# Four attention layers on one core: when the side work of the full layers is queued

## The chip, the cores and the metric

The kernel runs on one core of one Trainium2 chip. The metric is the device time of one execution in microseconds (us); the kernel before was executed three times for its time and once more under the hardware profiler. The core has engines that run at the same time, each with its own instruction queue: PE (TensorE, matrix products into PSUM), ACT (ScalarE, here mostly exponentials), DVE (VectorE), POOL (GpSimd) and SP (SyncE, which issues nearly all DMAs).

## The reference

The input x is 2048 x 512 in float32. Four layers follow each other, each with layer norm, 32 heads of 16, softmax attention, an output projection and a residual sum:

```python
x = A_x
x = x + _A_ref(_layernorm(x, axis=-1), A_wqkv, A_wo)
x = x + _B_ref(_layernorm(x, axis=-1), B_wqkv, B_wo)
x = x + _A_ref(_layernorm(x, axis=-1), A_wqkv, A_wo)
x = x + _B_ref(_layernorm(x, axis=-1), B_wqkv, B_wo)
return x
```

`_A_ref` (layers 0 and 2) lets each query see the 256 keys up to itself; `_B_ref` (layers 1 and 3, the full layers) lets it see all 2048. Both compute softmax(q k / 4) v per head and multiply by their output weights.

## The kernel before

**Score pairs.** A full layer walks through chunks of 512 queries (`c`, four of them) and head groups of four heads (`qd`, eight of them). For one chunk and head group it goes through 16 tiles `j` of 128 keys. For each tile, two score products (`exps`, L663; eight matmul instructions each) fill two PSUM buffers `s`, ACT takes the exponential of each (L671, 128 x 1024), and one tile later 16 products with the values (L715) add into `acc`. So a full layer has 1024 exponentials. When a head group ends, `epilogue` (L624 on) joins, transposes and divides the sums on DVE and POOL. Layer 1 takes the chunks in turn, each with eight head groups. Layer 3 is cut into blocks `(t, c)`: quarter `t` of the heads (two head groups) and chunk `c`, `t` in the outer loop; a block has 64 exponentials. The keys and queries of a head group are read back from DRAM when it begins (`load_full`: `kt` from `kf`, `qt` from `qs`).

**Side work.** Between score pairs PE does other matmuls, which prepare what comes later: projections of keys and queries (`keys`, `queries`, through `project`: twelve side matmuls per 128 output rows), values (`values`), output projections (`wo`, and in layer 3 `wo_part`: one head quarter of one chunk, four groups of three). In a full layer all of it goes through one PSUM tile, `halves`, because the other banks hold scores and sums. A side matmul is eight instructions (L360) and counts as `MM` = 0.222 us of PE; one for half of the heads' values counts as half.

**Squares.** Softmax needs no maximum here: a bound on the scores is taken from the sums of squares of keys and of queries. After the last matmul of a projection DVE joins the two halves (L374, L375), casts (L465, L466), POOL squares (L471), and two (or eight) small matmuls with `hsum` sum the squares over each head's rows (`squares`, L490) into `halves`. DVE then makes a maximum of them for keys (`km`, L509) or a row `m` for queries (L522, L523), which a DMA writes into `qs` (L535); the `qt` load of that chunk reads it. The squares of a finished projection are not emitted at once: a function is put on the list `pend` with a due time, and `settle` emits what is on the list, all of it or only what is due. In full layers `mms` (the function that emits a group of side matmuls) settles at its start, `key_shift` settles at its start (it needs the key maxima of all four chunks and writes the shift of the keys into `kf`), and the attention loop settles at the end of every block.

**The planner.** Python code decides where side work stands in the program, with an estimated clock `clock[0]`. Each piece of side work is a `Work` with a generator, a cost, dependencies and a name; output projections of layer 3 (`O3`) and the shift of the keys (`shift3`) have no name. `Side` holds a queue of them, and always takes the first one that is ready. In a full layer `share` is called once per key tile after the first of a head group, and once more inside the second: 16 calls per head group. It adds to a budget (cost left by steps left, at least `least`, up to 0.75) and lowers `lag`, and then emits side matmuls while the budget and the lag allow it and the clock is past `PH["free"]`. `mms` sets `PH["free"]` after a group, so that DVE has time to empty `halves`. A step, one key tile, counts as at least 1.8 us. At the end of a block of layer 3, `finish` emits everything that is still in the queue, whatever the budget. The works of the next block then form a new queue, with `carried` works (until now only preparations of weights) ahead of them. The queue of a block `(t, c)` is, in order: values of the upper heads (only in chunks 2 and 3 of the first quarter and in all four of the second), queries of chunk `c+1`, keys of chunk `c` for quarter `t+1`, in the last chunk the shift of the keys and the queries of chunk 0 for quarter `t+1`, and the output projection of the chunk before.

**Checks.** `verify` (queued in layer 1 as `CW`, after the fourth head group of the first chunk) makes sure that the weights are in a range for which the arithmetic holds. For each of eight matrices it loads four pieces into one buffer `wc` (L308), and DVE reduces each (L310); the waits between are the planner's.

**What sets the order.** Only PE executes in the order of the program text:

```python
ctx.enter_context(tc.manual_schedule(engines={mybir.EngineType.PE}))
```

For DVE, ACT, POOL and SP the compiler orders the instructions itself; earlier program text gives a higher priority, and `tc.high_priority` raises it further. On the chip every queue then runs strictly in the order that came out of this.

Of the kernel before, what the change touches and what calls it, by code (L numbers as in the profile page):

```python
# [19 lines left out]
P = 128  # L20
# [168 lines left out]
def fast_path(ctx, tc, flag, a_x, a_wqkv, a_wo, b_wqkv, b_wo, out):  # L189
# [29 lines left out]
    def wait(us):  # L219

        return "wait", clock[0] + us
# [80 lines left out]
    def verify(ty, s):  # L302

        am = vp.tile([P, D], F32, name=f"wa{ty}_{s}", tag="wa", bufs=1)
        for k in range(NC):
            f = slice(k * P, (k + 1) * P)
            raw = vp.tile([P, NC, P], F32, name=f"wc{ty}_{s}_{k}", tag="wc", bufs=1)
            nc.sync.dma_start(raw, mats[ty, s][:, f].rearrange("(k p) f -> p k f", p=P))  # L308
            yield wait(6)
            nc.vector.tensor_reduce(am[:, f], raw.rearrange("p k f -> p f k"), axis=AX.X, op=ALU.max, apply_absolute_value=True)  # L310
            yield wait(3)
        at = vp.tile([P, D], F32, name=f"wt{ty}_{s}", tag="wc", bufs=1)
        nc.vector.transpose(at, am)
        mx = vp.tile([P, D // 32], F32, name=f"wx{ty}_{s}", tag="wx")
        nc.vector.tensor_reduce(mx, at.rearrange("p (b r) -> p b r", r=32), axis=AX.X, op=ALU.max)
        nc.vector.tensor_tensor(wlow, wlow, mx, ALU.min)
        nc.vector.tensor_tensor(whigh, whigh, mx, ALU.max)
        yield wait(3)
# [29 lines left out]
    def mms(ps, pairs, after=1.6, us=MM):  # L348


        if PH["full"] and pend:
            settle()
            PH["free"] = clock[0] + 1.6
            yield 0.1
        for i, (a, b) in enumerate(pairs):
            if PH["full"]:
                for g in range(0, P, 32):
                    for r in range(2):
                        k = slice(R * r, R * r + R)
                        nc.tensor.matmul(ps[g:g + 32, r], a[k, g:g + 32], b[k], start=(i == 0), stop=(i == len(pairs) - 1),  # L360
                                         skip_group_check=True)
            else:
                nc.tensor.matmul(ps, a, b, start=(i == 0), stop=(i == len(pairs) - 1))  # L363
            spent(us)
            if i < len(pairs) - 1:
                if PH["full"]:
                    yield us
            else:
                PH["free"] = clock[0] + after
    TERMS = ((0, 0), (0, 1), (1, 0))  # L370

    def join(dst, ps, scale=1 / WS):
# [61 lines left out]
    def project(l, s, c, act, ht=None):  # L434


        ty, n = l % 2, f"{l}_{s}_{c}" + ("" if ht is None else f"_h{ht}")
        w = weights(ty, s, n, *((0, D) if ht is None else (ht * P, (ht + 1) * P)))
        yield wait(8)
        xc = XC[l, c]  # L440
        if s == 0:
            dst = rows(qs[ty, c])
        elif ty == 0:
            dst = rows(kw[c])
        else:
            dst = rows(kf)[:, :, c * QC:(c + 1) * QC]
        sqs = {}
        for t in range(NHT) if ht is None else (ht,):
            ps = bank()
            w0 = t * P if ht is None else 0  # L450
            yield from mms(ps, [(w[:, k, a, w0:w0 + P], xc[:, b, k, :]) for a, b in TERMS for k in range(NC)], 2.2)
            settle(not sqs)
            sp = vp.tile([P, 2, QC], F16, name=f"sp{n}_{t}", tag="sp", bufs=3)
            with tc.high_priority(HEAD_START):
                if PH["full"]:
                    j = vp.tile([P, QC], F32, name=f"j{n}_{t}", tag="j")
                    join(j, (ps[:, 0], ps[:, 1]))
                else:
                    if act:
                        nc.scalar.activation(sp[:, 0], ps, AF.Copy, scale=1 / WS)  # L460
                    else:
                        nc.vector.tensor_scalar(sp[:, 0], ps, 1 / WS, None, op0=ALU.mult)
                    nc.vector.scalar_tensor_tensor(sp[:, 1], ps, 1 / WS, sp[:, 0], op0=ALU.mult, op1=ALU.subtract)
            if PH["full"]:
                nc.vector.tensor_copy(sp[:, 0], j)  # L465
                nc.vector.tensor_tensor(sp[:, 1], j, sp[:, 0], ALU.subtract)  # L466
            sq = vp.tile([P, QC], BF16, name=f"sq{n}_{t}", tag="sq", bufs=NHT)
            if act:
                nc.scalar.activation(sq, sp[:, 0], AF.Square)
            else:  # L470
                nc.gpsimd.tensor_tensor(sq, sp[:, 0], sp[:, 0], ALU.mult)  # L471
            sqs[t] = sq

            d = dst[8 * t:8 * t + 8].rearrange("h (d b) n -> (h d) b n", b=4)
            if s:
                nc.sync.dma_start(d[:, 0:2], sp[:, 0:1].broadcast_to([P, 2, QC]))
                nc.sync.dma_start(d[:, 2], sp[:, 1])
            else:
                nc.sync.dma_start(d[:, 0:2], sp)
                nc.sync.dma_start(d[:, 2], sp[:, 0])  # L480
            yield -MM if PH["full"] else -12 * MM
        return sqs
# [17 lines left out]
    def keys(l, c, act, ht=None):  # L500
        sqs = yield from project(l, 1, c, act, ht)

        def rest():
            ph = squares(f"k{l}_{c}_{ht}", sqs)
            if l not in KM:
                KM[l] = vp.tile([P, NQ], F32, name=f"km{l}", tag="km", bufs=2)
            r = quarters(ht)
            with tc.high_priority(HEAD_START):
                nc.vector.tensor_reduce(KM[l][r, c:c + 1], ph[r], axis=AX.XY if PH["full"] else AX.X, op=ALU.max)  # L509
        pend.append((clock[0] + 3.6, rest))  # L510

    def queries(l, c, act, ht=None):
        sqs = yield from project(l, 0, c, act, ht)

        def rest():
            ph = squares(f"q{l}_{c}_{ht}", sqs)

            m = vp.tile([P, QC], F16, name=f"m{l}_{c}_{ht}", tag="m", bufs=1)
            if l % 2:
                r = quarters(ht)  # L520
                if PH["full"]:
                    nc.vector.tensor_scalar(m[r], ph[r, 0], -0.515, None, op0=ALU.mult)  # L522
                    nc.vector.scalar_tensor_tensor(m[r], ph[r, 1], -0.515, m[r], op0=ALU.mult, op1=ALU.add)  # L523
                else:
                    nc.vector.tensor_scalar(m[r], ph[r], -0.515, None, op0=ALU.mult)
            else:
                kx = vp.tile([P, 1], F32, name=f"kx{l}_{c}", tag="kx")
                nc.vector.tensor_reduce(kx, KM[l][:, max(c - 1, 0):c + 1], axis=AX.X, op=ALU.max)
                if PH["full"]:
                    nc.vector.tensor_scalar(m, ph[:, 0], kx, -0.515, op0=ALU.add, op1=ALU.mult)  # L530
                    nc.vector.scalar_tensor_tensor(m, ph[:, 1], -0.515, m, op0=ALU.mult, op1=ALU.add)
                else:
                    nc.vector.tensor_scalar(m, ph, kx, -0.515, op0=ALU.add, op1=ALU.mult)
            for t in sqs:
                nc.sync.dma_start(rows(qs[l % 2, c])[8 * t:8 * t + 8, 3, :], m[32 * t:32 * t + 8, :])  # L535
        pend.append((clock[0] + 3.6, rest))

    def settle(all_=True):
        while pend and (all_ or pend[0][0] <= clock[0]):
            pend.pop(0)[1]()  # L540
# [276 lines left out]
    class Side:  # L817
# [63 lines left out]
        def share(self):  # L881

            self.budget = min(self.budget + max((self.cost - self.spent) / max(self.steps - 3 - self.k, 1), self.least), 0.75)
            self.lag = max(self.lag - max(0.29, self.least), -0.3)
            while self.q and clock[0] >= PH["free"] and self.budget >= MM / 2 and (self.lag < 0.25 or self.budget > 0.45):
                c = self.one()
                if c is None:
                    break
                self.budget -= abs(c)
                self.lag += abs(c)  # L890

        def finish(self):

            prep = lambda w: w.name is not None and w.name[0] == "P"
            while any(not prep(w) for w in self.q):
                self.one(True)
            carried.extend(self.q)

# [13 lines left out]
    def attention(l, works):  # L912
# [5 lines left out]
        for t in range(NHT if l == 3 else 1):  # L918
            for c in range(NQ):
# [35 lines left out]
                    pvq[-1].append(lambda l=l, c=c, qd=qd, a=a: epilogue(l, c, qd, a))  # L955
                    ops = nxt
                if l != 1 or c == NQ - 1:
                    sd.finish()
                if not win:
                    settle()  # L960
        flush(0)
# [18 lines left out]
    def shift3(ht):  # L980
        def gen():
            key_shift(3, ht)
            yield -1e-6
        return Work(gen(), 0.0, None, [("K3", c, ht) for c in range(NQ)])

    def O3(c, ht):
        return Work(wo_part(c, ht), PO / 4, None, [("O", 3, c, ht)], True)
# [175 lines left out]
```

## Time and profile before

| | us |
|---|---|
| median of three runs | 2833.63 (2832.23 to 2835.97) |
| profiled execution | 2828.29 |
| its span | 2826.5 |
| layer 1's score pairs | about 511 to 1492 |
| layer 3's score pairs | about 1832 to 2809 |
| PE busy over the span | 2511.5 (89%) |
| ACT busy | 2373.8 (84%) |
| DVE busy | 1090.7 (39%) |
| POOL busy | 516.4 (18%) |

A line of the timeline has the start in us, the duration, the engine, the line of the kernel, the operation, what it writes from what it reads, and how many instructions were merged; in brackets stands how long the engine was idle before and what ended that. A line of waits names who waited for whom, then the total in us, how often, and the longest. A line of the stages has the window, its length, and busy us with the number of instructions for each engine, then the clock that was granted to PE as a share of full speed, the share of time in which the DMA engines were busy and GB/s. PE is busy for 89% of the span, but matmuls overlap and their ends are modelled, so that alone does not make it the bound.

### The profile page before, as it was taken

The page shows a single profiled execution, that of the slowest core. Times are in us where ns is not written, and L with a number is a line of the kernel's source. Part 1 is how long each engine was busy: PE and PEld are TensorE (multiplying, and loading weights), DVE is VectorE, ACT ScalarE, POOL GpSimd, SP SyncE. Part 2 cuts the span into 40 slices and gives each one's busy share as a digit, 9 for nine tenths or more (in the row PEclk, how much of TensorE's full clock was granted, in tenths as well). Part 3 has the DMA queues.
Part 4 walks back from the last instruction along what each step waited for, and adds up shares of the span by engine and source line. Part 5 has one row for each costly group of instructions (what it writes and reads, how often), then busy time and mean ns, then how long its engine had stood idle before and what let it go on. Part 6 is the DMA issues. An engine that isn't in the chain of part 4 may idle for free.

```text
span 2826.5 us, 112278 instructions
## 1 busy us (share of the span) xinstructions
PE 2511.5 (89%) x50513; PEld 1103.9 (39%) x50513; DVE 1090.7 (39%) x2314; ACT 2373.8 (84%) x2683; POOL 516.4 (18%) x1074
## 2 busy tenths in 40 slices
PE   7889989698999999999998888889999999988887
PEld 3233334343443444443343333534444443333332
DVE  5464466221333223322325566422433343333222
ACT  4565654599999999999995667399999999999997
POOL 1445541000100000100014678100000000000000
PEclk9999999899999999999999999999999999999999
DMA  8887867321223223222325464623334343333331
GB/s 288 228 230 238 244 200 205 126 78 59 95 88 97 81 91 105 84 68 76 107 78 167 146 188 137 171 65 101 109 112 119 112 120 109 103 104 107 105 98 55
DMA packets 335035, 359.67 MB, mean 127 GB/s; under 512 B 113616, under 2 KB 250320, under 8 KB 328144
## 3 DMA queue, kind: packets, MB, share of 16 engines
q1 hardware_dynamic: 334544, 352.40, 41.5%
q8 instruction: 397, 6.50, 1.0%
q14 instruction: 94, 0.77, 0.1%
HBM read 239.60 MB, written 96.99 MB: 119 GB/s over the span
## 4 chain that ended last, share of the span: by engine, by line
ACT 49%; PE 23%; issue 11%; DVE 8%; DMA 5%; POOL 3%; SPq 1%; ACTq 0%; POOLq 0%; DVEq 0%
ACT e L671 48%; PE b L363 9%; PE acc L715 3%; PE acc L748 3%; PE s L663 2%; PE b L360 2%; PE bs L363 2%; PE s L667 2%; DMA wc<-in_B_wqkv_dram 1%; POOL sq_h L471 1%; POOL e L738 1%; POOL e L741 1%; DMA wc<-in_A_wqkv_dram 1%; DVE wa L310 1%; DMA qt<-qs 1%
## 5 line engine op out<-in xcount | busy, mean ns | idle before, releaser
L671 ACT ACTIVATE e<-s 128x1024 f32<-128x1024 f32 (+2 forms) x2432 | 2249.7, 1048 | 165.1 <-PE s L667 103.7
L715 PE MATMUL acc<-e,vt 64*17 64x512 f32 x16384 | 1093.3, 591 | 1.2 <-DVE sa L375 1.2
L663 PE MATMUL s<-qt,kt 64*32 64x512 f16 x16384 | 859.6, 381 | 134.7 <-ACT e L671 102.8
L663 PEld LDWEIGHTS <-kt 64*32 64x32 f16 x16384 | 402.5, 89 | 917.9 <-issue 834.2
L715 PEld LDWEIGHTS acc<-e,vt 64*17 64x17 f32 x16384 | 283.3, 92 | 72.7 <-issue 4.7
L741 POOL TENSOR_SCALAR_AFFINE_SELECT e<-e 128x256 f32<-128x256 f32 x512 | 224.7, 445 | 194.7 <-ACT e L671 193.5
L738 POOL TENSOR_SCALAR_AFFINE_SELECT e<-e 128x256 f32<-128x256 f32 x448 | 198.7, 450 | 121.7 <-ACT e L671 120.0
L748 PE MATMUL acc<-e,vt 128*17 128x384 f32 (+2 forms) x2816 | 204.7, 397 | 8.2 <-POOL e L738 4.3
L650 POOL TENSOR_TENSOR oh<-o,oh 128x512 f16<-128x512 f32 x31 | 36.3, 1170 | 924.9 <-DVE oh L649 895.1
L374 DVE TENSOR_SCALAR sa<-acc 128x512 f32<-128x512 f32 x64 | 44.2, 691 | 403.1 <-PE acc L715 403.1
L667 PE MATMUL s<-qt,kt 64*128 64x384 f16 (+2 forms) x1408 | 129.1, 280 | 61.9 <-ACT e L671 37.8
L363 PE MATMUL b<-xc,w 128*128 128x512 f16 x696 | 165.2, 389 | 10.8 <-DMA w<-wd 7.9
L619 DVE SCALAR_TENSOR_TENSOR x<-b,x 128x512 f32<-128x512 f32 x122 | 84.4, 692 | 161.8 <-PE b L360 145.1
L471 POOL TENSOR_TENSOR sq_h<-sp_h 128x512 bf16<-128x512 f16 x27 | 39.7, 1471 | 514.3 <-DVE sp_h L465 514.3
L363 PEld LDWEIGHTS <-w 128*128 128x128 f16 x816 | 77.6, 100 | 131.2 <-issue 38.9
L460 ACT ACTIVATE sp<-b 128x512 f16<-128x512 f32 x58 | 34.7, 598 | 110.9 <-PE b L363 100.9
L360 PE MATMUL b<-xc,w_h 64*32 64x512 f16 x2592 | 115.3, 378 | 5.1 <-DVE km L509 3.9
L667 PEld LDWEIGHTS <-kt 64*128 64x128 f16 x1408 | 54.4, 95 | 165.5 <-issue 137.0
L360 PE MATMUL b<-wv,xc 64*32 64x256 f16 (+1 forms) x3456 | 98.2, 309 | 22.6 <-DVE vt L375 22.4
L374 DVE TENSOR_SCALAR j_h<-b 128x512 f32<-128x512 f32 x27 | 18.6, 690 | 253.2 <-PE b L360 230.8
L360 PE MATMUL b<-xc,w 64*32 64x512 f16 x2688 | 111.1, 376 | 1.8 <-DVE vt L375 0.9
L471 POOL TENSOR_TENSOR sq<-sp 128x512 bf16<-128x512 f16 x28 | 41.5, 1483 | 375.8 <-DVE sp L465 375.8
(136 smaller groups left out, 1889.6 us busy)
## 6 DMA issues: line engine op xcount, KB each, us to landing
kt<-kf SPq DMA_DIRECT2D x128, 512.0 KB
qt<-qs SPq DMA_DIRECT2D x128, 256.0 KB
xd<-x SPq DMA_DIRECT2D x96, 256.0 KB
x<-xd SPq DMA_DIRECT2D x96, 256.0 KB
w<-wd SPq DMA_DIRECT2D x22, 1024.0 KB
kt<-kw SPq DMA_DIRECT2D x64, 256.0 KB
qs<-sp SPq DMA_DIRECT2D x48, 256.0 KB
wo<-wd SPq DMA_DIRECT2D x12, 1024.0 KB
```

The lines of the kernel that those rows point to most:

```text
L360: nc.tensor.matmul(ps[g:g + 32, r], a[k, g:g + 32], b[k], start=(i == 0), stop=(i == len(pairs) - 1), skip_group_check=True)
L363: nc.tensor.matmul(ps, a, b, start=(i == 0), stop=(i == len(pairs) - 1))
L374: nc.vector.tensor_scalar(dst, ps[0], scale, None, op0=ALU.mult)
L471: nc.gpsimd.tensor_tensor(sq, sp[:, 0], sp[:, 0], ALU.mult)
L619: nc.vector.scalar_tensor_tensor(xs[i], p, 1 / WS, xs[i], op0=ALU.mult, op1=ALU.add)
L663: nc.tensor.matmul(ps[g:g + 32, h], kt[R * h:R * h + R, pr, kc + g:kc + g + 32], qt[R * h:R * h + R, pr], start=True, stop=True, skip_grou ...
L667: nc.tensor.matmul(ps[:, h, s0:s0 + wd_], kt[R * h:R * h + R, pr, kc:kc + P], qt[R * h:R * h + R, pr, qc:qc + wd_], start=True, stop=True)
L671: nc.scalar.activation(e[:, :, w0:w1], ps[:, :, w0:w1], AF.Exp, scale=SCALE)
L715: nc.tensor.matmul(acc[r][32 * h:32 * h + DH + 1, :], V[l, qd // 4, j // 8][k, j % 8, 4 * (qd % 4) + h, :], es_[h // 2][k, h % 2, :], star ...
L738: nc.gpsimd.affine_select(v, v, pattern=[[0, 2], [-1, P]], compare_op=ALU.is_gt, fill=0.0, base=0, channel_multiplier=1)
L741: nc.gpsimd.affine_select(v, v, pattern=[[0, 2], [1, P]], compare_op=ALU.is_ge, fill=0.0, base=0, channel_multiplier=-1)
L748: nc.tensor.matmul(a[32 * h:32 * h + DH + 1, q * P:(q + nb) * P], V[l, (4 * c + j) // 4][:, j % 4, 4 * qd + h, :], es_[h // 2][:, h % 2, s ...
```

## The change

Six things change, all but the first in the full layers only. The checks wait 16 instead of 6 units of the planner's clock between a load and its reduce. A side group settles at its start only what is due, no longer everything, and the pause after settling is 2.4 instead of 1.6. The pause after any side group is 0.8 longer. `project` no longer settles in a full layer. Squares fall due 6.4 instead of 3.6 after their projection. One call of `share` stops once it has emitted 1.5 `MM` or more, which means two whole side matmuls at most. In layer 3, works without a name stay in the queue at the end of a block, other than the last, and so go to the next block; the shift of the keys gets a name so that it does not.

```diff
@@ verify @@
-            yield wait(6)
+            yield wait(16)
@@ mms @@
-        if PH["full"] and pend:
-            settle()
-            PH["free"] = clock[0] + 1.6
+        if PH["full"] and pend and pend[0][0] <= clock[0]:
+            settle(False)
+            PH["free"] = clock[0] + 2.4
             yield 0.1
...
-                PH["free"] = clock[0] + after
+                PH["free"] = clock[0] + after + (0.8 if PH["full"] else 0.0)
@@ project @@
-            settle(not sqs)
+            if not PH["full"]:
+                settle(not sqs)
@@ keys, and the same in queries @@
-        pend.append((clock[0] + 3.6, rest))
+        pend.append((clock[0] + (6.4 if PH["full"] else 3.6), rest))
@@ Side.share @@
-            while self.q and clock[0] >= PH["free"] and self.budget >= MM / 2 and (self.lag < 0.25 or self.budget > 0.45):
+            s0 = self.spent
+            while (self.q and clock[0] >= PH["free"] and self.budget >= MM / 2 and (self.lag < 0.25 or self.budget > 0.45)
+                   and self.spent - s0 < 1.5 * MM):
                 c = self.one()
@@ Side.finish @@
-        def finish(self):
+        def finish(self, keep=False):
 
-            prep = lambda w: w.name is not None and w.name[0] == "P"
-            while any(not prep(w) for w in self.q):
+            stays = lambda w: (w.name is None and keep) if w.name is None else w.name[0] == "P"
+            while any(not stays(w) for w in self.q):
                 self.one(True)
             carried.extend(self.q)
@@ attention @@
-                    sd.finish()
+                    sd.finish(l == 3 and (t, c) != (NHT - 1, NQ - 1))
@@ shift3 @@
-        return Work(gen(), 0.0, None, [("K3", c, ht) for c in range(NQ)])
+        return Work(gen(), 0.0, ("S3", ht), [("K3", c, ht) for c in range(NQ)])
```

More of the change, by code (lines that the diff above doesn't have):

```diff
@@ L535, in rest @@
                 nc.sync.dma_start(rows(qs[l % 2, c])[8 * t:8 * t + 8, 3, :], m[32 * t:32 * t + 8, :])
-        pend.append((clock[0] + 3.6, rest))
+        pend.append((clock[0] + (6.4 if PH["full"] else 3.6), rest))
     def settle(all_=True):
```

## The prediction

> **What bounds the kernel now.** I read, in this order: the page, busy time by stage, ACT's waits in the two full layers, and timelines around single waits.
>
> ```profile
> span 2826.5 us, 112278 instructions
> 508.00:1506.00 998.00, 906.21 (x22644) 406.62 (x22643) 291.86 (x609) 954.09 (x1038) 64.90 (x57) 0.99 0.28 86
> 1826.00:2810.00 984.00, 882.56 (x21667) 391.79 (x21665) 310.59 (x579) 953.34 (x1029) 57.17 (x42) 1.00 0.34 103
> 1832.00:1891.20 59.20, 58.92 (x64) 1.00 0.22 65
> ```
>
> The stage rows give PE, PEld, DVE, ACT, POOL in turn; the edits act in these two stages alone, layer 1 and layer 3. ACT is busy for 954 of 998 us and 953 of 984 us, so the exponentials set the pace: the last row, ACT alone in one block of layer 3, has 64 of them in 59.2 us, 0.92 each. PE has a tenth to spare, and there the side matmuls go. What can be won or lost is ACT's waiting for scores. Its rows, in order of time (three windows of layer 1, all of layer 3, then the three places in layer 3 where a shift of the keys is made):
>
> ```profile
> ACT e L671 <- PE s L663: 22.1, 4, 12.6
> ACT e L671 <- PE s L663: 10.9, 12, 3.2
> ACT e L671 <- PE s L667: 5.6, 1, 5.6
> ACT e L671 <- PE s L663: 22.7, 30, 2.8
> ACT e L671 <- PE s L663: 3.8, 3, 2.8
> ACT e L671 <- PE s L663: 2.5, 1, 2.5
> ACT e L671 <- PE s L663: 1.9, 1, 1.9
> PE b L360 <- DVE vt L375: 2.9, 3, 1.1
> PE s L663 <- issue: 2.1, 2, 1.4
> ```
>
> Layer 1 loses 22.1 us before 556 us (the checks, below), 10.9 in its middle and 5.6 at its end, where leftover side work is run off. The last two rows are PE's own waits in layer 1's middle and in layer 3.
>
> **The change, part by part.** *Squares.* One squares event of layer 3, on all engines:
>
> ```profile
> 2104.76 0.41 PE L360 MATMUL b<-xc,w_h 64*32 64x512 f16 x8
> 2105.24 0.69 DVE L374 TENSOR_SCALAR j_h<-b 128x512 f32<-128x512 f32 x1 [13.76 <-PE b L360]
> 2105.97 0.69 DVE L375 SCALAR_TENSOR_TENSOR j_h<-b,j_h 128x512 f32<-128x512 f32 x1
> 2106.69 0.43 DVE L465 CAST sp_h<-j_h 128x512 f16<-128x512 f32 x1
> 2107.15 0.69 DVE L466 TENSOR_TENSOR sp_h<-j_h,sp_h 128x512 f16<-128x512 f32 x1
> 2107.28 1.45 POOL L471 TENSOR_TENSOR sq_h<-sp_h 128x512 bf16<-128x512 f16 x1 [23.23 <-DVE sp_h L465]
> 2108.79 0.39 PE L490 MATMUL b<-sq_h,hsum 64*32 64x512 bf16 x2 [0.93 <-POOL sq_h L471]
> 2109.22 0.68 DVE L522 TENSOR_SCALAR m<-b 32x512 f16<-32x512 f32 x1 [0.78 <-PE s L663]
> 2109.53 1.94 ACT L671 ACTIVATE e<-s 128x1024 f32<-128x1024 f32 x2 [0.51 <-PE s L663]
> 2111.37 0.29 SPq L535 DMA_DIRECT2D qs<-m  x1
> 2112.75 0.37 SPq L684 DMA_DIRECT2D qt<-qs  x1
> 1632.28 3.22 DMA qt<-qs
> 1542.95 6.11 DMA qt<-qs
> ```
>
> The last projection matmul ends at 2105.17; join, cast and POOL's square take until 2108.73, so the squares can run 3.6 us after it. They are queued earlier, PE waits 0.93 us and ACT 0.51. The new due time, 6.4 us after the projection is retired, which itself is a pause after its last matmul, puts them some 10 us behind it, so these waits go wherever another side group follows. In layer 1 that is 10.9 less the 2.9 of value joins and 0.6 of one other join: 7.4. In layer 3 it is 22.7 less 8.2 at the shifts, 2.1 of instruction issue and some 2 that no squares stand before (the layer's start, the head groups' starts): 10.4. The shifts stay, because the key shift still empties the list at once. Together **-18** (ends -18 and 0: a gain can't exceed the waits).
>
> *Checks.* The wait of 6 becomes 16:
>
> ```profile
> L310 DVE TENSOR_REDUCE wa<-wc x32: 1017/1040/1104, 355.6 to 550.4; 128x128 f32<-128x512 f32 x32
> 525.61 1.02 DVE L310 TENSOR_REDUCE wa<-wc 128x128 f32<-128x512 f32 x1 [2.65 <-DMA wc<-in_B_wqkv_dram]
> 526.54 0.41 DVE L374 TENSOR_SCALAR vt<-b 128x256 f32<-128x256 f32 x1
> 527.47 1.27 PE L360 MATMUL b<-wv,xc 64*32 64x256 f16 x40 [6.84 <-DVE vt L375]
> 529.29 1.02 ACT L671 ACTIVATE e<-s 128x1024 f32<-128x1024 f32 x1 [7.44 <-PE s L663]
> 529.41 1.07 DVE L310 TENSOR_REDUCE wa<-wc 128x128 f32<-128x512 f32 x1 [2.00 <-DMA wc<-in_B_wqkv_dram]
> ```
>
> A check's reduce waits for its load, the join of values stands behind it on DVE, PE waits for the join, ACT for PE: the 22.1 us. But the code appends the checks only after four of eight head groups of layer 1's first chunk, and all 32 ran between 355.6 and 551 us, before that place. DVE and SP do not keep the program's order; whatever is ready fills their gaps, and the checks come last in priority before and after. So I take **0**, near the row that shows them hoisted; ends -22.1 (they move away) and +3.8 (one more check, 529.41 less 525.61, ahead of a join).
>
> *Longer pauses after a group* (+0.8). A planner step is at least 1.8 us, so the next call comes 1.6 to 1.8 us after a group's end, which both pauses refuse, and the one after it at 3.3 or more, which both allow; at a head-group boundary the next call is at 3.07, still past 3.0. I cost it at nothing; without that 0.07, each boundary would lose a call.
>
> *Two side matmuls per step, and output projections kept over.* Layer 3 gives the side queue 32 calls per block (two head groups of 16 calls). Before and after, in calls: values 9 and 10 (three or four quarter-size matmuls a call instead of up to five); a query or key projection 7 and 7 (twelve matmuls at two, and a pause); an output projection 8 and 12, because a group of three no longer fits one call: 2, then 1, then the pause. Settling costs 1 call before and 2 after, since 2.4 us is longer than a step. Six blocks in a row have one of each and the values, 480 instructions of L360 each (the first and third of them below: 24 value pieces and 36 others, eight instructions a piece):
>
> ```profile
> 1951.60:2012.20 60.60, 15.14 (x480) 7.51 (x480) 1.00 0.31 94
> 2076.30:2137.70 61.40, 16.11 (x480) 8.20 (x480) 1.00 0.35 106
> ```
>
> Before: 9+7+7+8+2 = 33 for 32 calls, the last group forced at the block's end. After: 10+7+7+12+4 = 40. What is over now stays queued; carried work is added to the next block's queue *first*, and the projections behind it may not stay. Going through the blocks: the one at 1951.6 leaves two groups (6 calls); the next has 6+10+7+7 before its output projection begins, and leaves three groups (9); the one at 2076.3 then has 9+10+7+7 = 33, so the key projection fills the last call and a whole output projection (12) is over; from the fourth on 12+10+7+7 = 36, and some four matmuls of a key or a query projection are forced at the end. The blocks of the third head quarter have no values and work the rest off. An output projection that moves takes along its weight load, four loads and four stores of x on SP and eight adds on DVE; five buffers for its input and four for x cover one that is over, and SP is idle between the DMAs shown above, so I cost that at nothing (two over would run out of x buffers and stop the third's loads).
>
> The queries of the next block, or their squares, so come at the very end: a settling needs a group that starts after the due time, and none does, so they wait for the settling at the block's end. In front of the next block's first score now stands the whole chain above: 0.43 to m, 2.15 to its DMA, 1.38 until qt's load is issued, 3.22 for that load (the nearer of the two rows: one 256 KB load, as here; 6.11 is the other end), 0.41 for eight score matmuls: 7.6. Two score buffers hold at most two exponentials, 1.84 us, less the 0.4 that the second's scores take: ACT is covered for 1.4 and waits 6.2. Behind the waiting score on PE stand the last value products, and behind those the epilogue. PE also cools:
>
> ```profile
> 520.60:527.40 6.80, 0.03 (x7) 0.00 (x0) 2.77 (x4) 1.25 (x2) 0.00 (x0) 0.80 0.20 57
> 527.40:531.60 4.20, 4.13 (x96) 2.18 (x103) 1.08 (x2) 1.20 (x2) 0.00 (x0) 0.51 0.22 64
> 1316.20:1318.90 2.70, 0.02 (x6) 0.00 (x0) 1.75 (x2) 0.23 (x1) 2.68 (x2) 1.00 0.17 56
> 1318.90:1323.80 4.90, 4.86 (x82) 1.81 (x89) 1.44 (x2) 2.92 (x3) 0.00 (x0) 0.65 0.18 61
> 531.42 6.52 ACT L671 ACTIVATE e<-s 128x1024 f32<-128x1024 f32 x7 [1.11 <-PE s L663]
> 1492.31 2.78 PE L360 MATMUL b<-wv,xc 64*32 64x512 f16 x96 [1.54 <-DVE vt L375]
> ```
>
> After 6.8 us without matmuls the granted clock was 0.51 for 4.2 us, and ACT lost 1.11 more: I add 1.0 per start. The Trainium skill, page "TensorE: Matmul & The Clock Gate", section "Part 1: The HAM clock gate", says that an idle window of about 3.4 us halves the clock until about as long a busy stretch; the trace agrees after 6.8 us, but here 2.7 us were enough (0.65 afterwards). By the page's window an estimate is half of 3.4, 1.7 per start, which would make the sum 3.5 us longer.
>
> The five starts: 7.2 at the one that now lies at 2076.3; 8.2 at the next, where the key's join (2.6 us of DVE) partly stands ahead of m; 9.1 and 9.1 for the next two, with four forced matmuls (0.23 each from the row of 96) ahead; 11.7 for the one after, whose query is itself forced and must wait 3.6 for its square. **+45.3**; ends 0 (all settled in time) and +60 (qt at 6.11).
>
> *Layer 1's end.* Longer settling costs seven calls and the steps after them catch up at two; I take six more matmuls run off, **+1.4** (ends 0 and +4).
>
> Sum: -18+0+45.3+1.4 = +28.7. Where rounding lets four value pieces through in a call, a block gains a call or two and its start is some 2 us cheaper; I take 2.7 off: **+26**. The profiled execution took 2828.29 us (span 2826.5), so 2854; the median of the runs is 2833.63, 5.3 above it: **2860 us**.
>
> **The rivals.** *The squares are won and the overrun costs nothing* (faster). For it: only a query settled later than about 6 us before its block meets the chain, and the event above settles at 2108.79 the query of the block that starts at 2137.7, 29 us ahead; the forecast takes all of that away. It decides if Q's squares still land four calls ahead. Then -18+1.4: **2817**. *The checks move after all*: +26-22.1, **2838**; against it the row of 355.6 to 550.4. With both, 2795. *The starts are dearer* (qt at 6.11, clock slow on top): **2880**. *The change does not do what it says*: for the checks that is the forecast.
>
> **Chances.** Forecast 0.62 (own range 2840 to 2876); squares alone 0.17; checks move 0.11, both 0.03; dearer 0.07. 0.2%, 5.7 us, is about what a measurement here can tell. Slower: most of the forecast, the dearer case, some of the moved checks, 0.71; same 0.07; faster 0.22. Leaving out both together and the far ends, the range is 2813 to 2878.
>
> **What would show it.** Right: PE hardly waits for POOL's square in layer 3, ACT has waits of 6 to 12 us at four or five block starts of layer 3 with a qt load before them, checks still run from about 355 to 551 us, key shifts still cost some 8 us. Wrong: no wait for qt at block starts, or checks spread over layer 1.

## The result and the profile after

| | before | after |
|---|---|---|
| median, us | 2833.39 (2832.23 to 2835.97) | 2871.30 (2864.42 to 2878.59) |
| ratio | 1 | 1.0133 (95% interval 1.0105 to 1.0161) |
| profiled execution, us | 2828.29 | 2868.51 |
| its span, us | 2826.5 | 2866.8 |
| layer 1, first to last exponential, us | 979.7 | 969.1 |
| layer 3, first to last exponential, us | 975.5 | 1020.6 |

(The median of before is over four runs here, the three of the table above and one more.) The change makes the kernel slower, by 37.9 us in the median and by 40.2 between the two profiled executions. Layer 1 became 10.6 us shorter and layer 3 became 45.1 us longer. What remains is 3.8 us ahead of layer 1, 2.2 between the last exponential of layer 1 and the first of layer 3, and -0.2 at the end. The 3.8 us can't be given to the change: in the profiled executions below that leave the checks where they are, layer 1 begins anywhere from 508.0 to 520.8 us. Layer 3 has a spread too: in the four kernels below whose layer 3 is that of before it lasts 978.2 to 981.4 us, so the 975.5 of before is a short one. In the changed kernel most lines stand one to three further down: L672 is the exponential, L664 the scores of a full layer, L491 the sum of squares, L523 and L524 the row `m`, L536 its DMA, L685 the `qt` load.

First, ACT's waits for scores, in the same order as those shown of before: the first chunk of layer 1, the rest of layer 1, its end with the start of layer 2 (before: 16.0 us in such a window, in the second fence), and all of layer 3. The last three rows are waits of PE in layer 3.

```profile
ACT e L672 <- PE s L664: 21.3, 3, 14.8
ACT e L672 <- PE s L664: 4.5, 7, 1.1
ACT e L672 <- PE s L668: 18.5, 6, 8.1
ACT e L672 <- PE s L664: 74.3, 31, 10.6
PE s L664 <- DMA qt<-qs: 29.4, 6, 5.9
PE b L491 <- DVE m L524: 9.2, 4, 2.6
PE b L491 <- POOL sq_h L472: 4.6, 4, 3.7
```

Of before, ACT's waits at layer 1's end and PE's waits for POOL's squares in layer 3:

```profile
ACT e L671 <- PE s L667: 16.0, 6, 5.6
PE b L490 <- POOL sq_h L471: 14.4, 26, 2.3
```

The first chunk has kept its 22 us. The middle of layer 1 went from 10.9 to 4.5. In layer 3 the waits for squares fell from 26 to 4, and in their place six waits for a `qt` load have come, a kind that the list of before did not have. ACT's waits in six windows of layer 3, each around the start of one block, hold most of the 74.3 us:

```profile
ACT e L672 <- PE s L664: 8.2, 3, 6.1
ACT e L672 <- PE s L664: 9.1, 3, 7.6
ACT e L672 <- PE s L664: 11.2, 4, 9.0
ACT e L672 <- PE s L664: 12.2, 4, 9.8
ACT e L672 <- PE s L664: 12.9, 3, 10.6
ACT e L672 <- PE s L664: 12.2, 4, 10.3
```

They sum to 65.8 us. The blocks begin at 1892.4, 2081.8, 2152.2, 2223.6, 2297.3 and 2371.5; the last five are those that the prediction names, by before's times 2076.3 to 2325.6. Here is the chain of work through the fifth of the six, the start at 2297.3, with start, duration and what it was, a row for each piece:

```profile
2285.47 0.91 PE b L360 x32
...
2286.40 0.70 DVE j_h L374
...
2287.13 0.70 DVE j_h L375
...
2287.87 0.41 PE b L491 x2
...
2288.37 0.69 DVE m L523
...
2289.08 1.00 DVE sp_h L467
...
2290.10 0.69 DVE m L524
...
2290.81 2.94 DMA qs<-m
...
2293.76 2.68 DMA qt<-qs
...
2296.58 0.63 PE s L664 x7
```

Four side matmuls (32 instructions) of a key projection were forced at the block's end. DVE joins the keys, only then can PE sum the squares of the *queries* into the same PSUM tile, DVE makes `m` in two steps, between which a step for the keys stands, a DMA writes `m`, and the load of the next block's queries follows it. The first score matmul comes 11.1 us after the first forced one.

### The profile page after: what moved, and what is told of

Read it like the earlier page. It is cut to its first block, busy times and chain, and to the rows that moved or that the text cites. A ratio compares the mean times of both kernels' runs of the same rounds, so it can differ in the third digit from the quotient of the medians.

```text
span 2866.8 us, 112292 instructions
## 1 busy us (share of the span) xinstructions
PE 2527.5 (88%) x50513; PEld 1104.4 (39%) x50513; DVE 1087.9 (38%) x2314; ACT 2365.6 (83%) x2683; POOL 513.1 (18%) x1074
## 4 chain that ended last, share of the span: by engine, by line
ACT 52%; PE 22%; issue 11%; DVE 7%; DMA 6%; POOL 2%; SPq 1%; ACTq 0%; DVEq 0%; POOLq 0%
ACT e L672 51%; PE b L363 8%; PE acc L716 3%; PE acc L749 3%; PE bs L363 2%; PE s L664 2%; PE b L360 2%; PE s L668 2%; DMA wc<-in_A_wqkv_dram 1%; DMA qt<-qs 1%; DVE wa L310 1%; POOL e L739 1%; DMA wc<-in_B_wqkv_dram 1%; POOL e L742 1%; DVE ot L635 0%
## 5 line engine op out<-in xcount | busy, mean ns | idle before, releaser
L672 ACT ACTIVATE e<-s 128x1024 f32<-128x1024 f32 (+2 forms) x2432 | 2241.4, 1057 | 211.5 <-PE s L668 108.3
L664 PE MATMUL s<-qt,kt 64*32 64x512 f16 x16384 | 854.2, 382 | 163.2 <-ACT e L672 105.0
L664 PEld LDWEIGHTS <-kt 64*32 64x32 f16 x16384 | 405.9, 90 | 980.2 <-issue 900.3
L360 PE MATMUL b<-wv,xc 64*32 64x256 f16 (+1 forms) x3456 | 99.2, 308 | 23.2 <-DVE vt L375 21.6
L374 DVE TENSOR_SCALAR j<-b 128x512 f32<-128x512 f32 x28 | 19.3, 691 | 258.4 <-PE b L360 258.4
L360 PE MATMUL b<-wo,oh 64*32 64x512 f16 x2592 | 111.6, 378 | 5.2 <-DVE x L620 4.4
```

Source lines behind the costliest of these rows:

```text
L374: nc.vector.tensor_scalar(dst, ps[0], scale, None, op0=ALU.mult)
L664: nc.tensor.matmul(ps[g:g + 32, h], kt[R * h:R * h + R, pr, kc + g:kc + g + 32], qt[R * h:R * h + R, pr], start=True, stop=True, skip_grou ...
L672: nc.scalar.activation(e[:, :, w0:w1], ps[:, :, w0:w1], AF.Exp, scale=SCALE)
```

## The experiments

Each kernel ran in rounds beside the kernel before on the same chip, and the ratios are against those runs. The kernel before had medians of 2835.8 to 2836.9 there, with single runs between 2829 and 2843, so the ratios, and not the medians, are to be compared with the 1.0133 above.

**The change without the cap.** In `share` the term `and self.spent - s0 < 1.5 * MM` is left out.

> The changed kernel without the limit of two side matmuls per call; everything else of the change stays, so output projections are still carried over. Theory (it takes the cap and the carrying together to make the queue of a block too long; what costs is a block's first scores waiting for queries that were settled at the end of the block before): the planner now settles three of the five late queries' blocks only partly, so the starts that lay at 2081.8 and 2152.2 become normal and save their 9.4 and 11.8 us; the starts of the blocks behind (1,1), (2,1), (3,1) of the second quarter stay late at up to 12 us each. 2871 - 21 = about 2850. Rival A (the cap alone makes the work too long): all five starts normal, 2871 - 60 = 2811. Rival B (carrying alone does it): no change, 2871.

Measured: 2840.15 us, ratio 1.0012 (1.0002 to 1.0022). The waits of ACT and of PE for `qt` in its layer 3:

```profile
ACT e L672 <- PE s L664: 47.1, 26, 7.9
PE s L664 <- DMA qt<-qs: 21.2, 4, 8.2
```

The theory is right in kind: without the cap the carrying costs far less, and it is not free. The blocks were named wrongly. Late in full were the starts of the second block, of the first block of the second quarter and of the first block of the third (first waits of 6.0, 7.9 and 7.5 us); at the three between ACT waited 3.2 us at most for its first score. By the order of the program a key projection that spills over forces its own matmuls, but the queries ahead of it are settled when it starts; no row is shown for that.

**The change without carrying.** `sd.finish()` is called as before, and everything left is forced at the block's end; the cap stays.

> The changed kernel without carrying: finish empties the whole queue at the end of each block, the cap stays. Theory: without work ahead of them in the queue all queries but those of the layer's first block are settled in time, five late starts (59.8 us in the profile of the changed kernel) go; some 44 more matmuls of output projections are forced at block ends, 0.22 each, 10 us: 2871 - 60 + 10 = about 2821. Rival A (the cap is enough to make the queries late): 2860 to 2871. The start of the second block of layer 3, late by 8.6 us, stays.

Measured: 2840.84 us, ratio 1.0012 (1.0001 to 1.0023). ACT's and PE's waits in layer 3, and then the timeline at the start of the block (1,1):

```profile
ACT e L672 <- PE s L664: 43.4, 19, 5.9
PE b L360 <- DVE x L620: 15.4, 10, 1.5
PE s L664 <- DMA qt<-qs: 4.3, 1, 4.3
```

```profile
2135.99 0.84 PE L360 MATMUL b<-wo,oh 64*32 64x512 f16 x24 [1.53 <-DVE x L620]
...
2138.36 1.48 PE L360 MATMUL b<-wo,oh 64*32 64x512 f16 x24 [1.54 <-DVE x L620]
...
2140.40 1.03 ACT L672 ACTIVATE e<-s 128x1024 f32<-128x1024 f32 x1 [4.95 <-PE s L664]
```

The five late queries are gone, one `qt` wait is left, as the theory has it. But I had priced the forced output projections by their matmuls alone. Two forced groups of three stand behind each other here, and each must wait until DVE has emptied the one PSUM tile, 1.54 us. ACT loses 4.95 us where 1.3 of matmuls were counted. In all of layer 3 PE's waits for these adds are 15.4 us, against 4.3 in the kernel before, so they are a part of the 20 us by which the expectation missed, and the rest stays open (the profiled execution, 2830.49 us, is the fastest of the ten). So under the cap, what does not fit is paid at the block's end in one way or the other. Without the start of the second block (8.2 in the changed kernel, about as much here) ACT's waits in layer 3 are 66 us with carrying and 35 without. Against the kernel with neither (0.9983, below) the cap costs 0.3% without carrying and 1.5% with it, so the carried way is the dearer one.

**The change without the later squares.** `mms` and `project` settle everything as before, due 3.6, pause 1.6; cap, carrying and the longer pause stay.

> The changed kernel with the squares handled as before (settled at the start of the next side group, due 3.6, pause 1.6, and within project); cap, carrying and the longer pause stay. Theory (late settling is a part of the cause beside the long queue): the queries of four of the five blocks are settled when the key projection behind them starts, only the key squares are left for the block's end, where PE waits for their join and POOL square, about 3 us each; only the start of the block behind (3,1) is late in full, 12 us; the first block's start is normal. Squares wait as before. 2833 + 12 + 4 x 3 + 1 = about 2858. Rival (the long queue alone makes every start late): five starts of 12 on top of the squares' waits, about 2890.

Measured: 2853.89 us, ratio 1.0065 (1.0048 to 1.0082), the forecast within 4.

```profile
ACT e L671 <- PE s L663: 53.2, 30, 10.4
PE b L490 <- POOL sq_h L471: 26.5, 25, 3.7
PE s L663 <- DMA qt<-qs: 10.7, 2, 5.8
```

Only the start of the block behind the second quarter's last one is late in full (ACT waits 10.4 us for its first score); at the four ahead of it the first wait is 4.5 to 5.4, for a forced key projection whose POOL square PE waits for. So the long queue alone does not make five queries late. It takes squares that wait for a group which starts late enough as well.

**Neither cap nor carrying.** Both edits above together; the later squares, the longer pause and the checks' wait remain.

> The changed kernel without the cap and without carrying: only the later squares, the longer pause and the checks' wait remain. Theory: no late start but that of the second block of layer 3 (8.6 us, the first block has no output projection behind its projections, so nothing settles them before its end); the squares' waits are gone as in the changed kernel; 19 more forced matmuls, 4 us. 2871 - 60 + 4 = about 2815, faster than the kernel before by 18. Rival (later squares win little, the rest of the 2871 is not the starts): 2830 to 2840.

Measured: 2829.36 us, ratio 0.9983 (0.9968 to 0.9998), a gain of 5 where 18 was expected.

```profile
ACT e L672 <- PE s L664: 31.6, 17, 5.9
PE b L360 <- DVE x L620: 9.2, 6, 1.5
PE s L664 <- DMA qt<-qs: 4.3, 1, 4.3
```

The squares' waits are gone (2.2 us of PE waiting for POOL's squares, against 14.4 before), but 9.2 us of PE waiting for the adds of forced output projections (4.3 before), and the late second block, take most of that back: ACT's waits in layer 3 are above the 22.7 of before, layer 3 is as long as before (976.8 us), and what was won stands in layer 1 (971.8 against 979.7). The number is that of the rival, and its first half, that the later squares win little, holds for this kernel. Its second half, that the rest of the 2871 is not the late starts, falls: they went and 1.5% went with them.

**The change without `m`'s DMA.** In layer 3 the row `m` is not written, so queries take another bound from what layer 1 left there.

```diff
             for t in sqs:
-                nc.sync.dma_start(rows(qs[l % 2, c])[8 * t:8 * t + 8, 3, :], m[32 * t:32 * t + 8, :])
+                if ht is None:
+                    nc.sync.dma_start(rows(qs[l % 2, c])[8 * t:8 * t + 8, 3, :], m[32 * t:32 * t + 8, :])
```

> The changed kernel without the DMA that writes the queries' row m into qs in layer 3 (left out: the loads of the queries then take what layer 1 left in that row, so the softmax is shifted by another bound); all matmuls, squares and joins stay where they are. It takes the end of the chain away from the late starts: the load of the queries no longer stands behind the square sums, m and m's DMA. Theory (a late start is the chain projection, squares, m, its DMA, load): the first late start, at 1885 in the changed kernel, nearly vanishes (its projection is long done, only two settlings on PE are left, 2 us), the other five keep join, cast, square on PE and the load that still waits for the projection itself, and lose m and its DMA, 3 to 4 us each: 2871 - 6 - 5 x 3.5 = about 2848. Rival (the starts are late because of the matmuls and squares forced into PE at the block's end, not because of the load): no change, 2871.

Measured: 2839.11 us, ratio 1.0006 (0.9992 to 1.0020), a gain of 1.3% over the changed kernel, somewhat more than expected.

```profile
ACT e L673 <- PE s L665: 45.7, 28, 8.4
...
PE s L665 <- DMA qt<-qs: 5.4, 2, 3.8
```

All matmuls, squares and joins were still there, and PE still waited 9.2 us for `m` between two settlings, but the waits for `qt` fell from 29.4 to 5.4 us and ACT's from 74.3 to 45.7. So nearly half of the price of the late starts is the end of the chain, the row's DMA and the load behind it; the rest is forced matmuls and squares on PE. Least went at the last of the six, whose own projection is forced: its first wait fell from 10.3 to 8.4 us.

**The checks' wait alone**, `wait(16)` for `wait(6)` in the kernel before.

> The kernel before with the one edit of the checks (16 instead of 6 units between load and reduce). Theory: a wait of the planner moves text, and DVE and SP do not follow the text where work is ready, so the 32 reduces still run from about 356 to 551 us and the time is that of the kernel before, 2836 within 6. Rival: some reduces move behind 560 us and the first chunk gains, 2815 to 2825.

Measured: 2836.46 us, ratio 1.0002 (0.9991 to 1.0013): nothing. The reduces of the checks in the changed kernel, then in this one:

```profile
L310 DVE TENSOR_REDUCE wa<-wc x32: 1017/1046/1096, 358.3 to 553.7; 128x128 f32<-128x512 f32 x32
```

```profile
L310 DVE TENSOR_REDUCE wa<-wc x32: 1015/1039/1094, 358.9 to 554.8; 128x128 f32<-128x512 f32 x32
```

**No checks**, the works `CW` left out of the kernel before.

> The kernel before without the checks of the weights (left out: the eight verify works; the final flag then says nothing of the weights). Theory: the 22.1 us that ACT loses before 556 us are the reduces of the checks, which wait on DVE for their loads ahead of the joins of the values; they go, and with them part of the DMA work of layer 0: 2836 - 22 = about 2815. Rival (the join of the values is late for another reason, such as the slow loads of layer 0's end): 2830 or more.

Measured: 2788.50 us, ratio 0.9833 (0.9804 to 0.9862), 48 us and not 22. ACT's waits for scores from 490 to 640 us, 23.1 in the kernel before, are now:

```profile
ACT e L671 <- PE s L663: 1.0, 1, 1.0
```

In the profiled executions, which lie 38.9 us apart, layer 1's length falls by 24.4 us (979.7 to 955.3), and layer 1 begins 16.6 us earlier (494.1 against 510.7): the checks also hold up the end of layer 0, in which they begin at 355.6 us. This kernel leaves out the loads with the reduces, so the two have no price of their own.

**Checks held back by data.** In the kernel before, each check's load waits for `lmin`, which every epilogue updates; in the second kernel each reduce does so too.

```diff
+            nc.vector.tensor_copy(raw[:, 0, 0:1], lmin[:, 0:1])
             nc.sync.dma_start(raw, mats[ty, s][:, f].rearrange("(k p) f -> p k f", p=P))
-            yield wait(6)
+            yield wait(20)
+            nc.vector.tensor_copy(am[:, f.start:f.start + 1], lmin[:, 0:1])
             nc.vector.tensor_reduce(am[:, f], ...
```

The first kernel has the first added line alone, the second all of it.

> The kernel before, with one copy of an element of lmin into each check's buffer ahead of its load. lmin is updated by every epilogue, so the load of a check can't start before the epilogue that stands last before it in the program; this makes by data what the longer wait was to make by order. Theory (DVE and SP do not keep the order of the text, only a dependency moves the checks): the 32 reduces run after about 600 us, one to three per head group, layer 1's first chunk loses its 22 us, a reduce may still hold DVE for its load's 2 us now and then: 2836 - 15 = about 2821. Rival: the reduces stall the joins there as they do at the start, 2836.

> As gate, and each reduce too waits for lmin, by a second copy into its output, with 20 instead of 6 units between load and reduce, so that most reduces stand behind a later epilogue than their load. Theory: hardly a reduce waits for its load, 2836 - 20 = about 2816; rival: same as gate, since a reduce of about 1 us that doesn't wait costs nothing anyway.

Measured: 2843.19 us, ratio 1.0026 (1.0012 to 1.0039), and 2810.03 us, ratio 0.9911 (0.9887 to 0.9935). The reduces of the first and ACT's waits from 640 to 1500 us there, then the reduces of the second and its waits in the same window:

```profile
L311 DVE TENSOR_REDUCE wa<-wc x32: 1019/1080/1101, 621.3 to 1025.9; 128x128 f32<-128x512 f32 x32
...
ACT e L672 <- PE s L664: 58.2, 26, 9.7
```

```profile
L312 DVE TENSOR_REDUCE wa<-wc x32: 977/1006/1103, 619.5 to 1439.4; 128x128 f32<-128x512 f32 x32
...
ACT e L673 <- PE s L665: 22.9, 17, 3.3
```

Only data moved the checks. In both kernels layer 1 begins as early as without the checks (495.0 and 492.9 us). Held back at the load alone they then do in the middle of layer 1 what they did at its start: the reduce stands on DVE, waits for its load (70.5 us in all, against 62.4 in the kernel before), and the joins behind it wait with it; layer 1 becomes 26.9 us longer. Only with the reduce held back as well (20.3 us of such waits) are 27 us won. For the first kernel the rival was right. For the second the number is near the theory's, but the theory looked for the gain in layer 1's first chunk, and in the profiled executions 17.8 us are won ahead of layer 1 and only 7.9 in it.

**The squares alone, repaired.** The later squares on the kernel before, with a pause of 1.6; a call of `share` settles what is due even if no group starts (`PH["open"]` is set while a group stands unfinished in `halves`); the key shift comes behind the quarter's last query projection and settles only what is due.

```diff
+            if pend and pend[0][0] <= clock[0] and clock[0] >= PH["free"] and not PH.get("open"):
+                settle(False)
+                PH["free"] = clock[0] + 1.6
+                return
...
-                a += [shift3(t + 1), Q3(0, t + 1)]
+                a += [Q3(0, t + 1), shift3(t + 1)]
```

> The kernel before with the later squares alone (due 6.4, only what is due is settled, pause 1.6), settled also by a call of share that starts no group, where halves is not in use, so that the first block's queries don't wait for its end; and the key shift behind the last query projection of a quarter, with only what is due settled. No cap, no carrying, no longer pause, no change of the checks. Theory: none of the six late starts; against the kernel without cap and carrying (2829) the second block's start wins 6 and the three key shifts another 4: about 2819, 17 below the kernel before. Rival: the forced output projections at the block ends (0.9 to 2.2 us each) and the added settling calls eat the gain, 2830 or more.

Measured: 2819.68 us, ratio 0.9938 (0.9921 to 0.9955), 16 below the kernel before. PE's waits for `qt` in its layer 3:

```profile
PE s L667 <- DMA qt<-qs: 7.1, 2, 3.8
```

The number is the theory's, the way to it is not. Two of the six starts are still late, those of the first blocks of the second and the third quarter: ACT waits 4.3 and 3.9 us for their first scores, for which it did not wait in the kernel before. ACT's waits in layer 3 (24.2 us, shown below) are no less than before. In the profiled execution, the slowest of the four (2829.63 us), layer 1 is 7.5 us shorter than before and layer 3 is 4.8 us shorter.

**Squares and checks together**, and then also with a larger least budget per call in layer 3, the opposite of the cap:

```diff
-... 0.34 if l == 3 and t < 2 else 0.0)
+... 0.42 if l == 3 and t < 2 else 0.0)
```

> The squares of squares_only and the checks of gate2 (loads and reduces held back by copies from lmin) together. Theory: the two act in different places (waits for squares in layers 1 and 3, layer 0's end and layer 1's first chunk), so their gains add: 17 + 27 below 2836, about 2792. Rival: checks that now stand in layer 1's middle hold the joins ahead of the squares, and the squares' gain in layer 1 (6 to 7) is lost: 2799 or more.

> squares_gate2 with a larger least budget per call in the first two quarters of layer 3 (0.42 instead of 0.34), the opposite of the cap: by the planner's count the values then take fewer calls and no output projection is forced at the end of a block. Theory (a block's queue is limited by calls, and what doesn't fit is paid at the block's end): the waits of 1 to 2 us at the six block ends go, 2781 - 6 = about 2775. Rival (more matmuls between two score pairs delay the scores by as much as is won): 2781 or more.

Measured: 2781.31 us, ratio 0.9814 (0.9796 to 0.9831), and 2771.64 us, ratio 0.9777 (0.9763 to 0.9790). ACT's waits in layer 3, with the squares alone, with both, and with the larger budget:

```profile
ACT e L675 <- PE s L667: 24.2, 22, 4.3
```

```profile
ACT e L677 <- PE s L669: 21.8, 23, 4.1
```

```profile
ACT e L677 <- PE s L669: 12.6, 15, 1.4
```

The gains of the first two add, and by more than their sum (55 against 16 and 27). In the profiled executions the extra 11 or 12 stand in layer 1: with both it is 28.8 us shorter than before, with one of them 7.5 and 7.9, and ACT's waits from 640 to 1500 us are 6.1 us against the 22.9 of the checks alone. Why was not tested; the rival had expected the opposite there. The larger budget makes layer 3 another 9.9 us shorter, and the scores do not suffer. But the theory had the place wrong. At the starts of the second and the third quarter ACT waited 4.1 us each for its first score and now waits 1.1; at the other block starts behind the layer's first it waited 0.3 us at most with either budget. These two kernels beat both the kernel before and the changed one; the best is 2.2% below the kernel before.

## Why the prediction was right

The forecast was 2860 us, slower; the median is 2871.30, inside the range (2813 to 2878) and inside the forecast's own (2840 to 2876). Step by step:

- *The calls*: the count came true. In the blocks from 1953.4 on the changed kernel emits 432, 456 and 456 instructions of L360 instead of 480, so two groups of three side matmuls stay over, then one more, then one more, a whole output projection in all, as the prediction has it. The next three blocks have 480, and the four of the third quarter 312 instead of 288: there the rest is worked off.
- *The late starts* decided, at exactly the five blocks named and through the chain described. The price of each was low: 9.1, 11.2, 12.2, 12.9 and 12.2 us against 7.2, 8.2, 9.1, 9.1 and 11.7, in sum 57.6 against 45.3. Two sizes were off. What comes after the first wait cost 1.5 to 2.4 us per start (12.9 less 10.6 in the fifth), against the 1.0 added for a cold PE. And pieces of the chain were longer: the join of the keys stands ahead of the query's sums in full (1.4 us, with 0.5 to 0.9 of forced matmuls before it), where 1.0 was taken in part, and `m`'s DMA took 2.94 us in the fifth start until the `qt` load was issued, against 1.38 in the event that the prediction used. At the other starts it took 1.28 to 2.16, and the load itself was shorter than the 3.22 taken (2.40 to 2.90). The start at 2081.8 has another piece that the prediction put at nothing, the adds of an output projection: the sums of squares waited 1.54 us until DVE had emptied the one PSUM tile.
- *A sixth late start*, 8.2 us, was missed. The layer's first block has no output projection behind its key projection, so by the program no group starts after the due time and its queries are settled at its end. The prediction names that rule for the long blocks and did not apply it to the short one.
- *Squares, -18*: right within some us, as far as the rows can tell. In layer 3 ACT's waits outside the six starts are 74.3 less 65.8, 8.5 us, against 22.7 before: 14.2 gone, 3.0 of them at the key shifts (next point), which leaves 11.2 where 10.4 was forecast. In layer 1's middle 6.4 went (10.9 to 4.5), 7.4 forecast; but the kernel without the later squares waits 7.2 there, so some 2.7 are the squares' and the rest is that of the other edits or of chance. ACT's waits in layer 3 were 25.4 to 28.9 us in the four kernels whose layer 3 is that of before, so the gain there is uncertain by some us. Layer 3's growth of 45.1 is also 6.5 less than its waits' growth (51.6): the steps between exponentials became shorter where no wait row tells why.
- *Key shifts* did not keep their 8.2 us: the waits at those three places are now 1.8, 1.8 and 1.6, 3.0 less. The prediction let them stay.
- *Checks, 0*: right, by the rows and by the run with that edit alone.
- *Layer 1's end, +1.4*: the waits there grew from 16.0 to 18.5 and the way to layer 3 by 2.2.
- *The longer pause, 0*: no run has it alone.
- *Output projections over a block, nothing on SP*: right within 0.1 us at the one start where other loads stood in the way. At 2081.8 the `qt` load stood on SP behind a load of `x` that waited for a store of `x`, but `m`'s DMA, issued at 2076.64, would by the shortest of the others (1.28) not have released it before 2077.92, and it was issued at 2078.03.
- *The 2.7 taken off for rounding*: no start was cheaper than its term, so nothing shows it.

So the mechanism was right, and that the total is near is in part luck: the starts cost 65.8 and not 42.6 (45.3 less 2.7), 23 more, and 9 us more were won elsewhere than forecast. With the starts alone put right the forecast would have been about 2883, beyond the stated range. So the rival *the starts are dearer* (2880) was near in size, but not by its load: that took 2.40 to 2.90 us and not 6.11. The rival *the squares are won and the overrun costs nothing* was not run as it stands, with cap and carrying. The kernel with the repaired squares (2820 us) comes near its 2817 without either, and still has two late starts.

On the clock, the row first: in the window of the fifth start the granted clock was 0.64, with PE busy for 3.75 of 13 us, and 0.69 in the 8.5 us from 2297.0 on, when PE was busy again.

```profile
2285.00:2298.00 13.00, 3.75 (x76) 1.31 (x72) 5.38 (x7) 2.35 (x3) 1.04 (x1) 0.64 0.51 154
2297.00:2305.50 8.50, 8.00 (x144) 2.79 (x129) 4.11 (x10) 5.85 (x7) 0.00 (x0) 0.69 0.01 2
```

The estimate of 1.7 per start from the Trainium skill, page "TensorE: Matmul & The Clock Gate", section "Part 1: The HAM clock gate", was nearer to the 1.5 to 2.4 than the 1.0 that I took from one row of before. How much of that is the clock, and how much the value products that had piled up, was not separated.

## What to carry to other kernels

When a planner hands out work in calls, count calls and not microseconds: a limit per call makes a full queue overrun, and what matters then is *which* work falls over the edge and who waits for it. A small result that a DMA must carry before the next block can load belongs at the head of the queue, and squares or sums that wait for "the next group" need a rule for the case that no group comes. And check by the start times in the trace whether an engine follows the text at all, before moving text: only a dependency moved the checks here. Moving them was worth 27 us, leaving them out 48.

## What the runs showed that I had not expected

The checks' 32 reduces of 1.04 us each are 33 us of a DVE that is 39% busy, and the checks, loads and reduces together, cost 48 us of the whole. In the kernel before, between 300 and 560 us, DVE stood waiting in its queue for the loads of three of the eight matrices alone for 31.6 us (for all eight 62.4):

```profile
DVE wa L310 <- DMA wc<-in_B_wqkv_dram: 31.6, 11, 15.1
```

The same reduces held back by data at both ends cost 21.5 (2810.0 against 2788.5).

A load on SP's queue can lengthen the chain through data that has nothing to do with it. The clearest case is a late start in the kernel with the squares alone, repaired. Pieces of its chain there:

```profile
2070.26 3.20 DMA xd<-x
...
2073.48 0.32 SPq L421
...
2073.89 2.19 DMA qs<-m
...
2076.10 2.97 DMA qt<-qs
```

DVE had finished `m` at 2072.1 us, but its DMA was issued at 2073.89, 1.8 us later. Ahead of it on SP stands a load of `x` (L421), which waits for a store of `x` (3.20 us) of an output projection. At the other late start of that kernel it was 1.5 us in the same way.
